# A retention layer with a gated feed-forward behind it, on one core: a new order list for the same operations

## The chip, the core and the metric

The kernel runs on one core of a Trainium2 chip. The metric is device microseconds of one execution. The engines are called as in the profile: PE is the matmul engine (PEld its weight loads), DVE, ACT and POOL work elementwise, and SP only issues transfers here.

## What is computed

Cut from the reference:

```python
# q, k, v: (4 batches, 8 heads, 768 positions, 64)
gamma = 1.0 - 2.0 ** (-5.0 - np.arange(H))
for t in range(S):
    state = gamma[None, :, None, None] * state + np.einsum('bhd,bhe->bhde', k[:, :, t], v[:, :, t])
    y[:, :, t] = (1 / sqrt(D)) * np.einsum('bhd,bhde->bhe', q[:, :, t], state)
x = y.transpose(0, 2, 1, 3).reshape(B * S, H * D)        # 3072 x 512
xn = x / np.sqrt(np.mean(x * x, -1) + 1e-6) * rms_g
g = xn @ w_gate                                          # 512 -> 1536
return (g / (1 + np.exp(-g)) * (xn @ w_val)) @ w_out     # 1536 -> 512
```

The matmuls take bf16 operands and add up in float32; inputs and output are float32.

## The kernel before

The 768 positions are cut into six chunks of 128. Within a chunk and batch, attention is computed as masked scores, and what comes from earlier chunks goes through a state per batch, which each chunk but the last extends. The feed-forward then takes one chunk of all four batches (512 tokens).

Nothing in this kernel is ordered by a scheduler. Every step is a small named function, and a string, ORDER, lists the calls; the last loop (L784) walks through it. A word such as `V.3.3@A` is the step V of chunk 3 and batch 3 on ACT (D is DVE, P is POOL, S is SP), and the digits behind a slash are the PSUM banks it takes, of eight. Each engine executes its instructions in the order of the list and waits where an operand, or the bank or buffer of a result, isn't ready.

The steps, with c the chunk and b the batch:

- `Lq`, `Lk`, `Lv` load; on SP through the hardware queue as float32, on POOL through the software queue with a cast to bf16. `wg`, `wv`, `wo` load pieces of the weights on POOL. Loads of chunk 2 wait for the piece `wo.8` (L327 to L338).
- `Cq`, `Ck` cast q and k, `V` scales v by a decay; on ACT a `V` is eight small instructions, one for each head. `Tq`, `Tk` transpose on PE and `Eq`, `Ek` copy the result out of PSUM (helper L152); for chunk 0 some of them pick rows of a packed layout (L381). From chunk 2 on `tq` and `tk` transpose by a transfer on SP instead (L402).
- `A` is the scores (L418, two array halves of 64 rows), `P` the same with the state's part, `M0` and `M1` apply the mask on DVE, `Y` makes the output rows. `S`, `R`, `N` are the RMS norm (ACT, POOL, DVE), `X` and `XE` its transpose on PE and the copy; `XE@S` is a transfer (L516).
- `J` and `D` make the decayed k, `K` is the state's update (eight products of 64x64, L541, result kv_ps), `U` adds it to the state, `B` casts the state to bf16.
- `g` and `v` are gate and value products (L564), `s` the silu on ACT, `h` the product of both on DVE. Chunk 5 has them in a form with seven products of half blocks (`ga`, `gb`, `gc`, `va`, `vb`, `vc`, L750), which needs sums of weights (`gS`, `vS`) and copies of an accumulator (`gq`, `vq`).
- The output product has the seven-product form in all chunks: `z1` to `z4` and `w1` to `w4` are sums, `a1`, `a6`, `a7`, `a4`, `b2`, `c5`, `c3` products (L660; accumulators a, b, c), `q1`, `q6`, `q7` copies of the accumulator a (tile sn), `r1` to `r4` the four quarters of the result and `s1` to `s4` their stores on SP (L688). An optional last number takes one half of the quarter.
- `H` and `hot` are filler matmuls, which no result uses (hot_ps), `G` and `GE` spread the norm's gain (g_row_ps, g_bc), `tab` is one small activation that brings ACT its table for silu, and `mk0`, `mk1`, `yd`, `vd`, `yt`, `mc` make masks and decays.

```python
    for w in ORDER.split():
        w, _, bk = w.partition("/")
        w, _, en = w.partition("@")
        f, *a = w.split(".")
        F[f](ENG.get(en), [int(i) for i in bk], *map(int, a))
```

Of the kernel before, what the change touches and what calls it, by code (L numbers as in the profile page):

```python
# [17 lines left out]
Lk.0.2@S H.8/0 Lk.1.1@S rms.1@S yt ident iota pick Lk.0.0@P Ck.0.2@D Lq.0.1@P Tk.0.2/1 vd Lq.0.0@P mk1 H.3/2 D.0.2@D  # L18
Lk.0.1@P mk0 Lq.0.2@P Lk.0.3@P Lq.0.3@P Tk.0.0/3 Lv.0.0@P H.1/4 Ek.0.0@D Tq.0.1/5 hot.3/6 Lv.0.1@P J.0.0/7 Eq.0.1@A
Tq.0.0/0 D.0.0@D Lv.0.2@P Eq.0.0@A Tk.0.1/2 Ek.0.2@D H.1/4 Ek.0.1@A Tq.0.2/3 Lv.0.3@P yd hot.2/6 A.0.0/5710 Eq.0.2@D  # L20
tab wg.0.2 G/4 M0.0.0 wv.0.2 M1.0.0 Tq.0.3/2 GE@A wg.2.4 M0.0.1 Tk.0.3/6 Eq.0.3@A Y.0.0/3 M1.0.1 Lq.1.1@P A.0.2/57
Ek.0.3@A H.3/4 M1.0.2 S.0.0 A.0.3/12 M0.0.2 R.0.0 H.1/0 M1.0.3 Y.0.2/6 wv.2.4 K.0.0/4 N.0.0 S.0.2 J.0.1/7 Y.0.1/0
# [796 lines left out]
```

## Time and profile before

| | before |
|---|---|
| times of three runs, us | 228.67, 230.32, 231.47 (median 230.32) |
| span of the profiled execution, us | 228.9 |
| the execution's own time outside the span | not given; the span stands for it |
| granted PE clock | 1.000 of full speed |
| PE busy | 219.0 us, 96% |
| DVE, ACT, POOL busy | 179.8, 98.1, 162.5 us |
| moved by transfers | 33.64 MB, 147 GB/s |
| instructions | 5499 |

Times are those of one profiled execution. A row of a view names the line of the kernel, the engine, the operation and its tiles (out<-in); "xN" is a count, and a bracket tells how long the engine waited ahead of it and for what.

### The profile page before, as it was taken

The numbers are of one execution on the slowest core, as the hardware profiler recorded it, in microseconds if no ns is written. First come the engines' busy times: TensorE is split into PE (matmuls) and PEld (weight loads), VectorE is DVE, ScalarE is ACT, GpSimd is POOL, SyncE is SP. The second block draws the span as 40 slices with busy tenths as digits, with TensorE's granted clock in tenths as the row PEclk, the third lists the DMA queues.
The fourth block names the chain that finished last, engine by engine and source line by source line (L and its number), as shares of the span: only waits on it lengthen the run. The fifth ranks groups of instructions, "written<-read, shape, count | busy, mean of one in ns | idle before, by whom it ended". The sixth has DMA issues, their size and how long they took to land.

```text
span 228.9 us, 5499 instructions
## 1 busy us (share of the span) xinstructions
PE 219.0 (96%) x2119; PEld 145.6 (64%) x2119; DVE 179.8 (79%) x325; ACT 98.1 (43%) x218; POOL 162.5 (71%) x214
## 2 busy tenths in 40 slices
PE   7799989999999999999999999999999999999991
PEld 2568744675447886446574448674457788888871
DVE  6599359889999968679747878791997789999850
ACT  7776342533247252362602424514335328754311
POOL 8979999658998979514584997886198899330800
PEclk9999999999999999999999999999999999999999
DMA  7999999999456888777989579469974432000254
GB/s 134 162 183 131 143 169 177 205 199 241 109 117 138 195 155 171 127 164 172 194 206 204 122 135 259 93 150 226 195 157 157 77 102 92 3 0 3 76 186 153
DMA packets 108171, 33.64 MB, mean 147 GB/s; under 512 B 94449, under 2 KB 108145, under 8 KB 108146
## 3 DMA queue, kind: packets, MB, share of 16 engines
q1 hardware_dynamic: 84674, 25.70, 49.8%
q0 software_dynamic: 23472, 7.60, 30.6%
q8 instruction: 16, 0.26, 0.4%
q14 instruction: 9, 0.07, 0.2%
HBM read 28.31 MB, written 6.29 MB: 151 GB/s over the span
## 4 chain that ended last, share of the span: by engine, by line
PE 59%; ACT 0%; DVE 0%; issue 0%
PE g_ps L564 14%; PE v_ps L564 14%; PE a L660 10%; PE c L660 6%; PE b L660 2%; PE ga L750 2%; PE va L750 2%; PE a_ps L418 1%; PE vc L750 1%; PE gc L750 1%; PE y_ps L456 1%; PE y_ps L460 1%; PE kv_ps L541 1%; PE vb L750 1%; PE gb L750 1%; ACT r L152 0%
## 5 line engine op out<-in xcount | busy, mean ns | idle before, releaser
L574 ACT ACTIVATE sg<-g_ps 128x512 bf16<-128x512 f32 (+2 forms) x64 | 35.9, 570 | 71.1 <-PE g_ps L564 63.2
L564 PE MATMUL g_ps<-xnT,wg_b 128*128 128x512 bf16 (+2 forms) x296 | 58.7, 339 | 0.9 <-ACT xnT L152 0.5
L564 PE MATMUL v_ps<-xnT,wv_b 128*128 128x512 bf16 (+2 forms) x296 | 59.2, 339 | 0.0
L586 DVE TENSOR_TENSOR hT<-sg,v_ps 128x512 bf16<-128x512 bf16 (+2 forms) x64 | 40.1, 647 | 18.7 <-PE v_ps L564 17.5
L564 PEld LDWEIGHTS <-wg_b 128*128 128x128 bf16 x296 | 25.3, 98 | 23.4 <-DMA wg_b<-in_moe_w_gate_dram 0.8
L564 PEld LDWEIGHTS <-wv_b 128*128 128x128 bf16 x296 | 25.6, 98 | 22.3
L660 PEld LDWEIGHTS <-hT 128*128 128x128 bf16 x288 | 27.6, 98 | 4.7
L633 POOL TENSOR_TENSOR z<-hT,z 128x512 bf16<-128x512 bf16 x14 | 16.9, 1218 | 12.7 <-PE a L660 6.7
L660 PEld LDWEIGHTS <-z 128*128 128x128 bf16 x216 | 20.8, 98 | 3.6 <-issue 0.7
L497 DVE SCALAR_TENSOR_TENSOR xn<-y_ps,rstd,g_bc 128x512 bf16<-128x512 f32 x22 | 16.5, 749 | 6.7 <-POOL rstd L485 6.5
L556 POOL CAST st_b<-st_f 64x256 bf16<-64x256 f32 x40 | 20.5, 513 | 1.4
L441 DVE TENSOR_TENSOR am<-a_ps,causal 128x512 bf16<-128x512 f32 x32 | 20.1, 680 | 1.6 <-PE a_ps L418 1.4
L473 ACT ACTIVATE xsq<-y_ps 128x512 bf16<-128x512 f32 x22 | 13.2, 600 | 16.1 <-PE y_ps L460 11.8
L660 PE MATMUL a<-wo_b,hT 128*128 128x256 bf16 x144 | 17.9, 273 | 0.0
L633 POOL TENSOR_TENSOR z<-z,hT 128x512 bf16<-128x512 bf16 x8 | 10.2, 1273 | 7.4 <-DVE z L633 3.8
L485 POOL TENSOR_TENSOR rstd<-ms,mhalf 128x1 f32<-128x1 f32 x24 | 13.7, 570 | 2.0
L483 POOL TENSOR_SCALAR ms<-ssq 128x1 f32<-128x1 f32 x24 | 4.7, 197 | 11.5 <-ACT xsq L473 10.3
L633 POOL TENSOR_TENSOR z<-hT 128x512 bf16<-128x512 bf16 x9 | 10.7, 1190 | 3.0 <-DVE hT L586 2.9
L683 DVE TENSOR_TENSOR r<-c,sn 128x512 f32<-128x512 f32 (+1 forms) x13 | 8.4, 645 | 5.5 <-PE c L660 4.4
L152 ACT COPY sn<-a 128x512 f32<-128x512 f32 x14 | 8.2, 583 | 10.5 <-PE a L660 10.5
L373 POOL TENSOR_TENSOR vp<-vf,vdec 128x512 bf16<-128x512 f32 x11 | 11.5, 1058 | 0.7 <-DMA vf<-in_v_dram 0.7
L441 DVE TENSOR_TENSOR am<-a_ps,mask 128x512 bf16<-128x512 f32 x16 | 10.1, 683 | 0.2 <-PE a_ps L418 0.2
(158 smaller groups left out, 396.0 us busy)
## 6 DMA issues: line engine op xcount, KB each, us to landing
out_dram<-r SPq DMA_DIRECT2D x22, 256.0 KB, 2.4
kf<-in_k_dram SPq DMA_DIRECT2D x18, 256.0 KB, 4.1
qf<-in_q_dram SPq DMA_DIRECT2D x16, 256.0 KB, 3.9
vf<-in_v_dram SPq DMA_DIRECT2D x16, 256.0 KB, 3.7
wo_b<-in_moe_w_out_dram POOLq DMA_DIRECT2D x3, 512.0 KB, 10.0
qb<-in_q_dram POOLq DMA_DIRECT2D x8, 128.0 KB, 5.6
vp<-in_v_dram POOLq DMA_DIRECT2D x8, 128.0 KB, 7.3
kb<-in_k_dram POOLq DMA_DIRECT2D x6, 128.0 KB, 5.1
```

The costliest lines, as they stand in the source:

```text
L373: e.tensor_tensor(out=u["vp"], in0=u["vf"], in1=vdec[:, c, :, None].to_broadcast([128, H, D]), op=ALU.mult)
L441: DVE.tensor_tensor(out=u["am"][:, i], in0=u["a"][i], in1=m, op=ALU.mult)
L473: ACT.activation(xsq, flat(u["y"]), AF.Square, accum_out=u["ssq"])
L485: POOL.tensor_tensor(out=u["rstd"], in0=ms, in1=mhalf, op=ALU.pow)
L497: DVE.scalar_tensor_tensor(out=u["xn"], in0=flat(u["y"]), scalar=u["rstd"], in1=g_bc, op0=ALU.mult, op1=ALU.mult)
L556: POOL.tensor_copy(st_b[b][r, :, i * 64:i * 64 + 64], st_f[b][r])
L564: nc.tensor.matmul(p[:, (n - n0) * m:(n - n0 + 1) * m], W[w][0][:, s, n * 128:(n + 1) * 128], xnT[c][:, s, b0 * C:b1 * C], start=s == 0, s ...
L574: ACT.activation(sg[:, :cols], done["wg", c, n0, b0][:, :cols], AF.Silu)
L586: DVE.tensor_tensor(out=h_of(c, r)[:, i:i + n1 - n0, b0 * C:b1 * C], in0=sg, in1=p, op=ALU.mult)
L633: e.tensor_tensor(out=x, in0=a, in1=b, op=how)
L660: nc.tensor.matmul(done[x, c][:, q], left(i, c, r)[:, k, q * C:q * C + C], right(i)[:, r, k], start=first and q == r == k == 0, stop=r == ...
L750: nc.tensor.matmul(p[:, q], l[:, r, q], m[:, k], start=first and q == k == 0, stop=q == k == 1, skip_group_check=True)
```

## The change

ORDER is replaced by another list. The functions, the loop and the tiles' rings stay. The list has the same steps once each, with one exception: the last accumulation of chunk 4's fourth quarter, its copy and its store (`a4.4.0.3`, `r4.4`, `s4.4`) come in two halves of two batches each. Some steps get another engine, among them `V` (two on ACT before, six after), `Ck`, `Cq`, `XE`, the weight sums and copies. Of the table the diff shows its last lines here:

```diff
-c3.5.2.3.1 r3.5.1 c3.5.2.3.0 r3.5.0 s4.5.1@S s4.5.0@S s3.5.0@S s3.5.1@S b2.5.2.3 r1.5 s1.5@S z4.4.1@P c3.4.0.3 r3.4
-s3.4@S a4.4.0.3 r4.4@A s4.4@S
+r2.4 c3.4.0.3 r4.5.1@A a4.5.2.3.0 r4.5.0@A s4.4.0@S s2.5@S s4.5.1@S s2.4@S z4.5.1@D c3.5.0.2 s4.5.0@S r3.4 c3.5.2.3.1
+r3.5.1 s3.4@S s3.5.1@S a4.4.0.3.1 r4.4.1@A s4.4.1@S c3.5.2.3.0 r3.5.0 s3.5.0@S
```

**State updates (`K`).** PE, where chunk 2's updates stand. kv_ps_1678 is that of `K.2.1` before; what follows it there is a product of chunk 0's output (c).

```order
L541 LDWEIGHTS kb_1353
L541 MATMUL kv_ps_1678<-vp_1597,kb_1353 64x64
L660 LDWEIGHTS z_985
L660 MATMUL c_1687<-w1_1254,z_985 128x256
L660 LDWEIGHTS z_985
L660 MATMUL c_1687<-w1_1254,z_985 128x256
```

PE at that place after: kv_ps_1760 is that of `K.2.3`, kv_ps_1785 that of `K.2.0`.

```order
L541 LDWEIGHTS kb_1381
L541 MATMUL kv_ps_1760<-vp_1422,kb_1381 64x64
L541 LDWEIGHTS kb_1321
L541 MATMUL kv_ps_1785<-vp_1613,kb_1321 64x64
L541 LDWEIGHTS kb_1321
L541 MATMUL kv_ps_1785<-vp_1613,kb_1321 64x64
```

Each of the twenty `K` stood alone among products of full size. From chunk 2 on they now stand in runs: `K.2.3 K.2.0 K.3.3 K.2.1 K.2.2`, then `K.3.2 K.3.1 K.3.0`, `K.4.3` and `K.4.2 K.4.1 K.4.0`; chunk 1's are `K.1.3 K.1.2 K.1.0 K.1.1`.

**The head.** ACT at the start, before, from the masks on. The rows of L302 are `tab`, the casts are copies of transposed q and k.

```order
L284 ACTIVATE mask_101<-row_m,nbias 128x128 x8
L152 CAST qT<-t_ps 128x512 x2
L152 CAST kT<-t_ps 128x512
L278 ACTIVATE ydec<-darg,lnscale 128x48
L302 ACT_TABLE_LOAD
L302 ACTIVATE warm<-zero 128x1
L152 COPY g_bc<-g_row_ps 128x512
```

ACT at the start, after; the rows up to the copy of g_bc, which is followed by more copies, squares and two copies of xnT before the second piece.

```order
L284 ACTIVATE mask_101<-row_m,nbias 128x128 x8
L278 ACTIVATE ydec<-darg,lnscale 128x48
L152 CAST kb<-kf 128x512
L152 COPY kT<-t_ps 128x512
L152 CAST kT<-t_ps 128x512 x2
L152 COPY g_bc<-g_row_ps 128x512
```

```order
L152 COPY xnT<-xt_ps 128x4x128 x2
L574 ACT_TABLE_LOAD
L574 ACTIVATE sg<-g_ps 128x256
L152 COPY kT<-t_ps 128x512
L574 ACTIVATE sg<-g_ps 128x384
```

The load of silu's table moved from the copies of the head to the place just ahead of the first silu (sg), since `tab` now stands in chunk 2. POOL at the start, before: the loads of v, then pieces of the weights among the norms (ms, rstd).

```order
L329 DMA vp<-in_v_dram 128x8x64 x4
L338 DMA wg_b<-in_moe_w_gate_dram 128x4x256
L338 DMA wv_b<-in_moe_w_val_dram 128x4x256
L338 DMA wg_b<-in_moe_w_gate_dram 128x4x256
L329 DMA qb<-in_q_dram 128x8x64
L483 TENSOR_SCALAR ms<-ssq 128x1
```

POOL at the same place after.

```order
L329 DMA vp<-in_v_dram 128x8x64 x4
L338 DMA wv_b<-in_moe_w_val_dram 128x4x256
L338 DMA wg_b<-in_moe_w_gate_dram 128x4x256 x2
L338 DMA wv_b<-in_moe_w_val_dram 128x4x256
L338 DMA wg_b<-in_moe_w_gate_dram 128x4x256
L338 DMA wg_b<-in_moe_w_gate_dram 128x4x384
L483 TENSOR_SCALAR ms<-ssq 128x1
```

Six pieces of the weights are issued ahead of the first norm, where there were three. On PE, 18 of the 20 `H` fillers now stand ahead of the first transposes; they were spread over the head.

**The end.** The last rows of PE before: two products of `c3.4` (c_3735), then the first of the twelve of `a4.4` (a_3687) that end the list.

```order
L660 LDWEIGHTS z_3574
L660 MATMUL c_3735<-wo_b_135,z_3574 128x256
L660 LDWEIGHTS z_3574
L660 MATMUL c_3735<-wo_b_135,z_3574 128x256
L660 LDWEIGHTS hT_2944
L660 MATMUL a_3687<-w4_1380,hT_2944 128x256
```

PE's last rows after: the second half of `a4.4` (a_3663) stands between the halves of `c3.5` (c_3822).

```order
L660 MATMUL c_3822<-wo_b_135,z_3858 128x256
L660 LDWEIGHTS hT_3147
L660 MATMUL a_3663<-w4_1354,hT_3147 128x256
L660 LDWEIGHTS hT_3147
L660 MATMUL a_3663<-w4_1354,hT_3147 128x256
L660 LDWEIGHTS hT_3116
L660 MATMUL a_3663<-w4_1354,hT_3116 128x256
L660 LDWEIGHTS hT_3116
L660 MATMUL a_3663<-w4_1354,hT_3116 128x256
```

SP's last stores before; r_3887 and r_3897 are halves of chunk 5's quarters, the last one is chunk 4's fourth quarter.

```order
L688 DMA out_0_dram<-r_3887 128x256 x2
L688 DMA out_0_dram<-r_3897 128x256 x2
L688 DMA out_0_dram<-r_3910 128x2x256
L688 DMA out_0_dram<-r_3927 128x2x256
L688 DMA out_0_dram<-r_3942 128x2x256
```

SP's last stores after; r_3959 is chunk 5's third quarter, r_3855 chunk 4's fourth.

```order
L688 DMA out_0_dram<-r_3921 128x2x256
L688 DMA out_0_dram<-r_3935 128x256
L688 DMA out_0_dram<-r_3955 128x2x256
L688 DMA out_0_dram<-r_3959 128x256
L688 DMA out_0_dram<-r_3855 128x256
L688 DMA out_0_dram<-r_3959 128x256
```

The last store was a whole quarter of 256 KB; it is a half now, and another half stands ahead of it. Between the head and the end, loads and attention of the later chunks stand earlier among PE's feed-forward products, and the stores of chunks 3 and 4 stand elsewhere among them.

More of the change, by code (lines that the diff above doesn't have):

```diff
@@ L17 @@
 ORDER = """
[L18 to L22, printed above, removed]
@@ L93 @@
-gs1.5.2 ga4.5.0 gs4.5.0 vq1.5.1@A gc3.5.0 gr3.5.0 h.5.0.2.0.2 va6.5.0 vq6.5.0@A ga7.5.1 gq7.5.1@A vb2.5.1/1 vr1.5.1
-vS3.1@P va1.5.2/6 gc5.5.1/4 gs3.5.0 vq1.5.2@A gr2.5.1 gs2.5.1 h.5.4.6.0.2 vb2.5.2/5 va6.5.1 vq6.5.1@A vr1.5.2 z1.4.1@D
-vS3.0@P va7.5.0 ga4.5.1 vc5.5.0/1 z2.4.2@P z4.4.2@P va6.5.2 z2.4.1@P gc3.5.1 va7.5.1 h.5.8.10.0.2 vq7.5.0@A vr2.5.0
-gr3.5.1 gs4.5.1 ga6.5.2 vc5.5.1/5 vq7.5.1@A vr2.5.1 va4.5.0 gs3.5.1 vc3.5.0 a1.5.0.2/0 h.5.2.4.2.4 va4.5.1 vr3.5.0
-a1.5.2.3 h.5.0.2.2.4 h.5.6.8.0.2 vc3.5.1 vr3.5.1 gq6.5.2@A z1.5.0@D vq6.5.2@A va7.5.2 vq7.5.2@A ga7.5.2 h.5.6.8.2.4
@@ L103 @@
-c3.5.2.3.1 r3.5.1 c3.5.2.3.0 r3.5.0 s4.5.1@S s4.5.0@S s3.5.0@S s3.5.1@S b2.5.2.3 r1.5 s1.5@S z4.4.1@P c3.4.0.3 r3.4
-s3.4@S a4.4.0.3 r4.4@A s4.4@S
+yt H.2/0 H.3/1 H.1/2 Lk.1.1@S rms.1@S vd Lq.0.0@P Lk.0.0@P H.8/3 H.3/4 ident pick Lk.0.2@S Lq.0.1@P iota mk0 H.1/5 G/6
+Lk.0.1@P Tq.0.0/7 causal Ck.0.2@D D.0.2@D Tk.0.2/0 Tk.0.0/1 Lq.0.2@P mk1 yd H.1/2 Eq.0.0@D Ck.1.1@A Ek.0.2@A Lk.0.3@P
+Ek.0.0@A Tq.0.1/3 Eq.0.1@D Lq.0.3@P J.0.0/4 D.0.0@D Tk.0.1/5 mc.1@P Ek.0.1@A GE@A hot.2/0 A.0.0/7213 M0.0.0 M1.0.0
@@ new lines @@
+g.0.2.3.0.3/2 s.0.3.4.0.3 R.0.3 N.0.3 s.0.0.2.2.3 v.0.3.4.0.3/3 K.0.3/1 Lq.1.1@P K.0.1/4 X.0.3/6 U.0.3@A XE.0.3@D
+g.0.5.6.0.3/0 g.0.4.5.0.3/1 s.0.2.3.0.3 v.0.2.3.0.3/2 h.0.3.4.0.3 g.0.0.2.1.2/6 g.0.0.4.3.4/3 h.0.2.3.0.3
+v.0.0.4.3.4/2 h.0.0.2.2.3 s.0.0.4.3.4 h.0.0.4.3.4 s.0.4.5.0.3 Tq.1.3/5 Eq.1.3@D g.0.4.6.3.4/3 v.0.4.5.0.3/1
+g.0.9.10.0.4/2 Lk.1.2@P Lk.1.0@P B.0.0 U.0.1@A Tq.1.0/4 s.0.4.6.3.4 s.0.0.2.1.2 h.0.0.2.1.2 v.0.4.6.3.4/3 Tq.1.1/5
+Tk.1.0/6 Lq.1.2@P h.0.4.5.0.3 wv.9.12 Eq.1.0@D h.0.4.6.3.4 g.0.11.12.0.4/7 Lk.1.3@P Eq.1.1@D B.0.3 Ek.1.0@A D.1.2@D
@@ new lines @@
+A.1.0/1436 M1.1.0 v.0.5.6.0.3/5 wg.6.9 Lv.1.3@P Lv.1.1@P mc.0@P Lv.1.0@P s.0.5.6.0.3 h.0.5.6.0.3 wv.6.9 B.0.1 M1.1.1
+M0.1.0 z1.0.0@D Tk.1.2/0 g.0.10.11.0.4/4 s.0.10.11.0.4 v.0.11.12.0.4/5 Tq.1.2/6 Eq.1.2@D Lv.1.2@P Tk.1.3/4
+v.0.10.11.0.4/1 s.0.9.10.0.4 Ek.1.2@A s.0.11.12.0.4 v.0.9.10.0.4/2 M0.1.1 h.0.11.12.0.4 wo.8.12 A.1.2/06 wo.4.8
+Ek.1.3@A A.1.3/73 M1.1.3 wo.0.4 M0.1.3 g.0.8.9.0.4/4 D.1.3@P Lk.2.2@S Y.1.1/5 S.1.1 M1.1.2 B.0.2 g.0.6.7.0.4/3
+h.0.10.11.0.4 Y.1.3/7 S.1.3 s.0.8.9.0.4 D.1.1@P R.1.1 s.0.6.7.0.4 g.0.7.8.0.4/6 Y.1.0/1 S.1.0 R.1.3 M0.1.2 Y.1.2/0
@@ new lines @@
+M0.3.0 R.3.3 Lv.5.1@S Lk.5.3@S a4.1.0.3 M1.3.0 tq.4.2 R.3.1 g.2.11.12.0.4/2 N.3.3 g.2.1.2.0.4/5 Lv.4.1@S Y.3.0/7 N.3.1
+s.2.1.2.0.4 Lq.4.0@S v.2.1.2.0.4/1 gS1.1@P h.2.1.2.0.4 z4.1.0@D S.3.0 R.3.0 N.3.0 Lk.4.3@S z4.1.2@P Cq.4.3@P
+v.2.10.11.0.4/0 tk.4.0 v.2.11.12.0.4/6 z1.2.1@P g.2.8.9.0.4/5 s.2.11.12.0.4 Ck.4.3@A h.2.10.11.0.4 XE.3.1@S
+v.2.3.4.0.4/1 c3.1.0.3 h.2.11.12.0.4 Cq.4.0@P B.3.3 s.2.8.9.0.4 K.3.2/2 K.3.1/7 XE.3.3@S K.3.0/0 U.3.2@D XE.3.0@S
+V.4.0@D V.5.1@A v.2.8.9.0.4/6 h.2.3.4.0.4 r3.1 XE.3.2@S v.2.9.10.0.4/5 g.2.9.10.0.4/2 s.2.9.10.0.4 vS1.1@P U.3.0@D
@@ new lines @@
+v.4.5.6.0.4/0 s4.2@S B.4.2 Y.5.2/3 S.5.2 R.5.2 h.4.7.8.0.4 v.4.9.10.0.4/1 a1.3.0.3/2 h.4.5.6.0.4 s.4.1.2.0.4
+c5.3.0.3/6 gS4.0@D b2.3.0.3/5 vS2.1@D N.5.2 XE.5.1@S z3.3.0@P h.4.1.2.0.4 z1.4.1@P z4.3.0@P z2.4.1@P vS4.1@D
+g.4.9.10.0.4/0 XE.5.2@S XE.5.3@S X3.5@P q1.3@D s.4.9.10.0.4 h.4.9.10.0.4 r1.3 ga1.5.1/4 ga1.5.0/3 a6.3.0.3 q6.3@A
+X1.5@P g.4.8.9.0.4/7 gq1.5.1@A v.4.8.9.0.4/0 s.4.8.9.0.4 gq1.5.0@A gS3.0@D h.4.8.9.0.4 gb2.5.0/1 gr1.5.0 gs1.5.0
+gS4.1@D gb2.5.2/5 vS4.0@D ga1.5.2/7 gq1.5.2@D gS3.1@D a7.3.0.3 q7.3@A gr1.5.2 z4.3.2@D v.4.2.3.0.4/0 gb2.5.1/1 gr1.5.1
@@ new lines @@
+X2.5@P ga6.5.0 gq6.5.0@A r2.3 h.4.2.3.0.4 z3.4.1@D gs1.5.1 a4.3.0.3 va1.5.0/5 z1.4.2@D z2.4.2@D gc5.5.0/1 ga7.5.0
+gq7.5.0@A gr2.5.0 s4.1@S c3.3.0.3 ga6.5.1 gs2.5.0 r3.3 va1.5.1/0 gq6.5.1@D gc3.5.0 gr3.5.0 X4.5@P vb2.5.1/6 ga4.5.0
+vq1.5.0@A ga7.5.1 vS3.0@P vb2.5.0/1 va6.5.0 r4.3@D vS3.1@P vq1.5.1@A gs1.5.2 gc5.5.1/2 vr1.5.1 h.5.4.6.0.2 gs3.5.0
+z4.4.2@P va1.5.2/6 gq7.5.1@A ga4.5.1 vq6.5.0@A vr1.5.0 va7.5.0 vb2.5.2/1 ga6.5.2 gs4.5.1 gr2.5.1 gs2.5.1 gc3.5.1
+h.5.0.2.0.2 gr3.5.1 vc5.5.0/4 vq7.5.0@A va6.5.1 gs4.5.0 gc5.5.2/3 vc5.5.1/2 vr2.5.0 h.5.2.4.2.4 vc3.5.0 vr3.5.0
@@ new lines @@
+h.5.0.2.2.4 gq6.5.2@A vq6.5.1@A va7.5.1 vq1.5.2@A vr1.5.2 z1.4.0@P vq7.5.1@A va6.5.2 z3.4.0@D z2.4.0@P z4.4.0@P s2.3@S
+z3.4.2@P gs3.5.1 va4.5.0 h.5.2.4.0.2 a1.4.0.3/4 ga7.5.2 gq7.5.2@A a1.5.0.2/1 ga4.5.2 vr2.5.1 q1.4@A vc3.5.1 va4.5.1
+gr2.5.2 z1.5.0@D h.5.8.10.0.2 gc3.5.2 vr3.5.1 vq6.5.2@A va7.5.2 vq7.5.2@A z2.5.0@P gr3.5.2 vc5.5.2/5 a1.5.2.3 a6.4.0.3
+h.5.6.8.2.4 b2.4.0.3/2 vr2.5.2 va4.5.2 h.5.4.6.2.4 z1.5.1@D q6.4@A z2.5.1@D vc3.5.2 z3.5.1@D gs2.5.2 h.5.10.12.2.4
+vr3.5.2 h.5.6.8.0.2 q1.5@A a6.5.0.2 gs3.5.2 h.5.8.10.2.4 z4.4.1@P z1.5.2@D z2.5.2@P z3.5.0@P a7.4.0.3 c5.5.0.2/3
```

127 lines of the change are left out of this document (52 added, 75 removed).

## The prediction
> **What bounds the kernel now.** I read the page's busy times first, then the stages, then who makes the matmul engine wait, then the chain that ended last.
>
> ```profile
> PE 219.0 (96%) x2119; PEld 145.6 (64%) x2119; DVE 179.8 (79%) x325; ACT 98.1 (43%) x218; POOL 162.5 (71%) x214
> PE 59%; ACT 0%; DVE 0%; issue 0%
> 30.00:40.00 10.00, 8.93 (x82) 4.34 (x80) 7.13 (x13) 3.38 (x6) 9.84 (x15) 1.00 1.90 172
> 40.00:50.00 10.00, 10.00 (x124) 6.54 (x123) 8.66 (x14) 5.30 (x13) 5.49 (x12) 1.00 1.21 196
> 190.00:200.00 10.00, 10.00 (x94) 8.96 (x93) 9.48 (x16) 8.55 (x17) 6.12 (x6) 1.00 0.16 54
> PE c L660 <- DVE r L683: 0.5, 1, 0.5
> PE kv_ps L541 <- DVE vp L373: 0.4, 1, 0.4
> ```
>
> In the stages, the first number behind the comma is PE's busy time. PE is the bound: from 40 us to about 220 us it is all but full, and the chain runs over PE for as far back as it was followed. PE takes its work in the order of the list. So the end is the sum of PE's slots, plus PE's waits, plus what follows PE's last matmul, and an edit on another engine counts only where PE waits for it. The two waits shown are the ones behind 40 us that are listed for PE's matmuls.
>
> **Tile forms.** K (kv_ps) and the A of attention run in array shapes other than 128x128. Here the chain has two K's among ordinary work (columns: start, length).
>
> ```profile
> 147.51 0.86 PE g_ps L564 x4
> 148.37 0.24 PE kv_ps L541 x8
> 148.62 0.97 PE v_ps L564 x4
> 149.59 0.24 PE kv_ps L541 x8
> 149.83 1.42 PE b L660 x12
> 151.25 1.31 PE c L660 x12
> 8.53 0.44 PE L381 MATMUL t_ps<-pick,qb 128*64 128x64 bf16 x16
> 8.91 0.44 PE L381 MATMUL t_ps<-pick,kb 128*64 128x64 bf16 x16
> ```
>
> Four wide matmuls take 0.86 alone and 0.97 behind a K, twelve products 1.31 alone and 1.42 behind a K. So a lone K costs 0.24 + 0.11 = 0.35 us. A run that stays in K's shape is seen in the last two rows: 16 matmuls from 8.53 to 8.91, which is 0.19 us for eight. A K directly behind another K should cost about that, 0.16 less. The 20 K's stand in 20 places before. After, the 16 from the second chunk on stand in five (runs of 4, 5, 3, 1 and 3), so 11 seams go: 11 x 0.16 = **1.8 us gained**. Bounds: 11 x 0.11 = 1.2 if only the slowed follower is saved, and 11 x 0.24 = 2.6 if a K in a run were nearly free.
>
> **The head, up to 40 us.** Here PE waits for first data and for copies.
>
> ```profile
> 1.11 3.34 PE L252 MATMUL hot_ps<-one 128*128 128x512 bf16 x8 [1.11 <-DVE one L165]
> 4.83 0.81 PE L252 MATMUL hot_ps<-one 128*128 128x512 bf16 x3
> 4.73 2.43 ACT L284 ACTIVATE mask<-row_m,nbias 128x128 f32<-128x128 f32 x8
> 9.49 0.59 ACT L152 CAST kT<-t_ps 128x512 bf16<-128x512 f32 x1
> 9.97 0.35 ACT L278 ACTIVATE ydec<-darg,lnscale 128x48 f32<-128x48 f32 x1
> 10.20 0.62 PE L418 MATMUL a_ps<-qT,kT 64*128 64x128 bf16 x16
> 10.32 1.28 ACT L302 ACT_TABLE_LOAD   x1
> 10.75 1.12 PE L311 MATMUL g_row_ps<-g_row,ones 1*128 1x512 f32 x2
> 16.87 0.63 ACT L152 CAST kb<-kf 128x512 bf16<-128x512 f32 x1
> 23.43 1.50 PE L564 MATMUL g_ps<-xnT,wg_b 128*128 128x128 bf16 x24 [0.47 <-ACT xnT L152]
> 31.84 1.04 PE L564 MATMUL g_ps<-xnT,wg_b 128*128 128x512 bf16 x4 [0.42 <-DMA wg_b<-in_moe_w_gate_dram]
> 33.53 0.40 PE L386 MATMUL t_ps<-ident,qb 128*128 128x128 bf16 x4 [0.65 <-ACT sg L574]
> 33.52 0.23 PEld L386 LDWEIGHTS <-qb 128*128 128x128 bf16 x4 [1.14 <-DMA qb<-in_q_dram]
> ```
>
> Two things get worse. First, 18 of the 20 big filler matmuls (hot_ps) now stand at the very start: eight slow ones to 4.5 and ten of about 0.2 us end near 6.6, and the g_row product (1.1) runs to 7.7. On ACT, masks to 7.2 are followed by ydec (0.35), a cast (0.63) and two kT copies (0.59 each), to about 9.6, since the second one's transpose ends near 8.9. J.0.0, which needs that copy, now stands on PE ahead of Tk.0.1: 9.6, J 0.25, the transpose 0.4, one more copy 0.6 and some hand-overs give a first A near 11.1 instead of 10.20, 0.9 late. Second, the table load (1.28) leaves its hidden place and stands directly ahead of the first silu, whose PSUM bank the second v product behind it wants: PE waits about 1.1.
>
> Two things get better. Five of the weight pieces and wg.9 are issued ahead of the first rstd pair on POOL, and all of chunk 1's q ahead of wv.9, so the DMA waits at 31.84 and 33.53 (0.42 and 0.65) should go, and with other work ahead the one at 23.43 (0.47). A matmul's row runs about 0.17 past its slot (1.04 here, 0.86 in the chain), so each gap really costs that much more: 1.54 + 3 x 0.17 = 2.0. Sum 0.9 + 1.1 - 2.0 = 0, and two seams fewer there: **-0.3 us**. Bounds: -2.0 (the new waits are covered) and +2.0 (the old ones stay).
>
> **The full stretch.** The wait for V.3.3 (0.4) should go: it stands behind two K's now. New waits come, because PE's order leaves less room. An example: the copy of an accumulator (sn) between product 7 and product 4 of one bank.
>
> ```profile
> 203.50 0.44 PE ga L750 x4
> 206.12 0.44 PE ga L750 x4
> L152 ACT COPY sn<-a 128x512 f32<-128x512 f32 x14 | 8.2, 583 | 10.5 <-PE a L660 10.5
> ```
>
> Before, ga7 ends at 203.9 and ga4 starts at 206.1: 2.2 us for a copy of 0.58. After, two products of 0.44 stand between: 0.87. Going through both lists with such durations I find some 30 places with under 0.9 us to spare, where before had four; none is short by itself, so only a busy queue makes PE wait there. Bounds 0 and +3 (0.1 at each); I take **+0.6**, somewhat over a wait like the two of before. With the -0.4: +0.2. Four V's more on ACT, eight small ACTIVATEs each, are some 8 us on an engine that is 43% busy: no term.
>
> **The end.**
>
> ```profile
> 220.35 0.42 DVE L683 TENSOR_TENSOR r<-c,sn 128x256 f32<-128x256 f32 x1 [1.38 <-PE c L660]
> 220.82 0.38 PE L660 MATMUL c<-wo_b,z 128*128 128x256 bf16 x2 [0.52 <-DVE r L683]
> 222.95 1.32 PE a L660 x12
> 224.30 0.58 ACT L152 COPY r<-a 128x512 f32<-128x512 f32 x1 [3.80 <-PE a L660]
> out_dram<-r SPq DMA_DIRECT2D x22, 256.0 KB, 2.4
> out_dram<-r SPq DMA_DIRECT2D x4, 128.0 KB, 1.7
> ```
>
> PE waits 0.52 between the halves of c3 of chunk 5, because r3.5.1 reads the bank that the second half writes. After, six matmuls of a4 (half of 1.32) stand between: **-0.5 us**. The last result was a whole one: copy 0.58, then 2.4 to landing. Now it is a half: 0.42, then 1.7; -0.9 at most. Another half store is issued just ahead, so I take **-0.8** (bounds -0.9 and 0, the latter if the stores queue). The Trainium skill, "DMA: Bandwidth & Descriptors", section "Anatomy of one DMA — SWDGE (gpsimd) path", speaks against much gain from halving: about 2 us are fixed and bytes cost 1 us per 436 KB, 0.3 us for 128 KB. By that the sum would be 0.4 less; it was fitted on the other path, and the rows here show 0.7.
>
> **Sum**: -1.8 - 0.3 + 0.2 - 0.5 - 0.8 = -3.2 us, from a span of 228.9 to 225.7. The median of the three times, 230.32, lies 1.4 above that span; carried over, **227.1 us**. A change under 1% (2.3 us) can't be told from none on this kernel.
>
> **Rivals.**
>
> *The gain is eaten* by the tight places: +3 instead of +0.6 leaves -0.8, 229.5 us. For it: DVE is 95% busy from 190 to 200 us. Against: one wait gives room to all behind it. Chance 0.20.
>
> *The change doesn't do what it says*: K's side by side still cost 0.35, since each has a bank of its own. Then -1.4 is left, 228.9 us. Against: the two transposes in a row also change banks. Chance 0.07.
>
> *SP's queue becomes the bound: slower.* By the PE work ahead of it, A.5.0 comes some 18 us sooner, while no load is fewer.
>
> ```profile
> SPq L329 <- DMA wo_b<-in_moe_w_out_dram: 46.1, 1, 46.1
> 79.98 7.05 SPq L516 DMA_TRANSPOSE xnT<-xn  x4
> 96.09 1.22 SPq L402 DMA_TRANSPOSE qT<-qb  x1
> ```
>
> SP's loads from chunk 2 on start when a piece of wo has landed, after a wait of 46.1 us, near 48.6. Until A.5.0 it issues 47 loads, 44 transposes and 7 stores. At some 0.6, 1.22 and 0.5 us that is 85 us; A.5.0 would stand near 154, 105 us later. If every transpose took the slow 1.76 (7.05 for four), it is 109 us and 4 us late; with the waits for casts between them PE would stand still at the last A's for some 8 us in all, 235 us. It decides where SP's issue and waits exceed 105 us. Against: wo's third piece is issued first now, which starts SP some 4 us earlier. Chance 0.08.
>
> *PE's clock falls in the head*, since the fillers leave the gaps from 9 to 17 us: the first rows of the head show 0.42 us for a slow filler. One stretch of 3.4 us at half speed would cost 1.7, 228.8 us. The Trainium skill, "TensorE: Matmul & The Clock Gate", section "HAM oscillation — how this bites in real kernels", sets this at idle gaps over about 3.4 us; no gap in my walk is over 1.2. Chance 0.03.
>
> *More is gained*: the head ends 2.0 ahead and nothing new waits, 224.8 us. Chance 0.15.
>
> **How the numbers follow.** The forecast has the remaining 0.47, from 225.6 to 228.8. The better cases reach down to 223.9 (K at its bound of 2.6 besides), the eaten gain up to 230.5 where tight places cost 4. Range **223.7 to 230.6**: outside lie the SP case and a little on either side. Faster by over 1% means under 228.0: 0.15, some 0.35 of the forecast and 0.06 of the rivals, **0.56**. Slower by over 1%, over 232.6: the SP case and 0.01 besides, **0.09**. Within 1%: **0.35**.
>
> **What would show it.** Right: K's in a run at about 0.2 us each; the table load just ahead of the first silu and a PE wait of about 1 us near 22; no DMA among PE's waits from 25 to 40; no wait between the halves of c3; 0.8 us less between PE's last matmul and the end. Wrong: PE waiting for transposed q or k behind 90 us, or waits of PE over 2 us in the full stretch.

## The result, and the profile after

The new list is slower: 238.07 us median (237.88 to 239.23, four runs) against 230.49 before (four runs, one more than the three of the 230.32 above); the ratio is 1.036, interval 1.031 to 1.041. The profiled execution took 238.14 us with a span of 236.4, so 7.5 us more span than before.

Busy times and the shares of the chain that ended last, of the page after:

```profile
PE 221.3 (94%) x2119; PEld 147.1 (62%) x2119; DVE 182.7 (77%) x324; ACT 107.3 (45%) x256; POOL 148.2 (63%) x206
PE 51%; DVE 19%; POOL 9%; DMA 9%; issue 6%; ACT 3%; SPq 2%; POOLq 0%; DVEq 0%; ACTq 0%
```

Before, the chain named PE and next to nothing else, but it was followed back only to about 89 us. After, it is followed to the start and half of it lies elsewhere. Part of that half is the head, which the chain of before doesn't reach, so the two shares can't be set side by side; behind 89 us too, though, it now passes through DMA, DVE and POOL. Where PE stands still, the busy time by stages tells; first before, then after (stretch, its length, then PE's busy time):

```profile
0.00:40.00 40.00, 35.71 (x485) 22.71 (x486) 28.89 (x77) 22.46 (x52) 36.90 (x62) 1.00 1.52 157
80.00:120.00 40.00, 39.59 (x368) 24.50 (x366) 28.89 (x49) 15.63 (x38) 24.52 (x38) 1.00 0.82 170
```

```profile
0.00:40.00 40.00, 36.32 (x490) 23.43 (x491) 26.97 (x74) 23.39 (x54) 37.91 (x65) 1.00 1.57 167
40.00:80.00 40.00, 39.62 (x391) 25.36 (x390) 36.46 (x59) 18.98 (x47) 29.12 (x38) 1.00 0.99 203
80.00:120.00 40.00, 38.53 (x339) 24.16 (x337) 28.42 (x48) 16.87 (x46) 22.12 (x34) 0.96 0.86 172
120.00:160.00 40.00, 37.44 (x330) 22.21 (x328) 29.59 (x52) 15.63 (x42) 25.16 (x38) 1.00 0.75 165
160.00:180.00 20.00, 19.66 (x147) 10.23 (x145) 15.40 (x26) 9.71 (x26) 6.75 (x14) 1.00 0.24 67
180.00:210.00 30.00, 27.32 (x230) 22.17 (x229) 27.51 (x39) 13.93 (x27) 20.65 (x17) 1.00 0.17 54
```

In the head PE is idle for 3.7 us instead of 4.3. From 40 to 210 us it was idle for 0.4 before, all of it in the stretch shown; after, it is idle for 0.4 + 1.5 + 2.6 + 0.3 + 2.7 = 7.4. What PE waits for, after (the rows that the text uses; others of up to 1.1 us are not shown):

```profile
PE gc L750 <- DVE vf L762: 1.2, 1, 1.2
PE a_ps L418 <- DMA qT<-qb: 1.1, 3, 0.6
PE g_ps L564 <- DMA xnT<-xn: 1.0, 1, 1.0
PE v_ps L564 <- ACT sg L574: 1.0, 1, 1.0
PE vb L750 <- DVE vf L762: 0.7, 1, 0.7
PE kv_ps L541 <- POOL vp L373: 0.6, 1, 0.6
PE va L750 <- DVE vf L762: 0.5, 1, 0.5
```

Three of these name what SP transposes (qT, xnT) or what stands behind a late load (vp), and three name the vector engine's sums of chunk 5 (vf); the wait for sg is one of the head. So behind the head there are two groups: one up to 160 us, one from 180 to 205.

**SP.** Its own instructions after, near the longest wait for xnT (start, length):

```profile
122.67 0.46 SPq L329 DMA_DIRECT2D qf<-in_q_dram  x1
123.17 0.72 SPq L329 DMA_DIRECT2D kf<-in_k_dram  x1
123.99 2.97 SPq L402 DMA_TRANSPOSE qT<-qb  x1
127.07 0.53 SPq L329 DMA_DIRECT2D qf<-in_q_dram  x1
127.69 0.53 SPq L329 DMA_DIRECT2D vf<-in_v_dram  x1
128.31 0.97 SPq L329 DMA_DIRECT2D kf<-in_k_dram  x1
```

Each starts about 0.1 us behind the end of the one before it. It is so from 44.3 to 159.5 us: 98 transfers, with one pause of over 0.3 (0.5). Before, pauses of over 0.3 add up to 14 us between 57 and 160. One of 1.6 us, from 90.2 to 91.8, in the same view of before:

```profile
89.25 0.94 SPq L329 DMA_DIRECT2D vf<-in_v_dram  x1
91.76 1.62 SPq L402 DMA_TRANSPOSE qT<-qb  x1
```

SP has become an engine that is always busy, though no page counts its issuing as busy time.

**The stretch at K.3.3.** PE and, below, ACT:

```profile
83.59 0.44 PE L541 MATMUL kv_ps<-vp,kb 128*64 128x64 bf16 x16
84.27 2.49 PE L541 MATMUL kv_ps<-vp,kb 128*64 128x64 bf16 x24 [0.23 <-ACT vp L371]
86.69 2.74 PE L660 MATMUL c<-wo_b,z 128*128 128x256 bf16 x12
```

```profile
83.35 0.62 ACT L152 CAST kb<-kf 128x512 bf16<-128x512 f32 x1 [3.54 <-DMA kf<-in_k_dram]
83.87 2.02 ACT L371 ACTIVATE vp<-vf,vdec 128x64 bf16<-128x64 f32 x8
```

V.3.3 stands on ACT behind a cast that waits 3.54 us for a load from SP, and K.3.3 gets its eight rows one by one, 0.24 apart. Three K's take 2.49 us, and the 12 products behind them take 2.74, where the same view has 1.47 for twelve (at 228.94, below): the stage from 80 to 120 us has a granted clock of 0.96, since the clock was halved for 3.4 us from 86.5 on. The stages count all this as busy, so it comes on top of the 7.4.

**DVE.** The sums of chunk 5's weights between 179 and 195 us, after, by kind:

```profile
L715 DVE TENSOR_TENSOR kf<-wv_b,vf 128x768 bf16<-128x768 bf16 x2 | 2.9, 1432 | 0.0
L715 DVE TENSOR_TENSOR wg_b<-wg_b 128x768 bf16<-128x768 bf16 x2 | 1.9, 966 | 0.0
L715 DVE TENSOR_TENSOR vf<-vf,wv_b 128x768 bf16<-128x768 bf16 x1 | 1.5, 1511 | 0.0
L715 DVE TENSOR_TENSOR kf<-wg_b,qf 128x768 bf16<-128x768 bf16 x2 | 1.4, 708 | 0.0
```

Seven sums, 7.7 us. Before, DVE had none of them in that stretch: POOL did five of the seven, from 53 us on, and DVE two at 131 and 176.

### The profile page after: what moved, and what is told of

Same layout as the page of the kernel before. It is cut to its first block, busy times and chain, and to the rows that moved or that the text cites. A ratio compares the mean times of both kernels' runs of the same rounds, so it can differ in the third digit from the quotient of the medians.

```text
span 236.4 us, 5515 instructions
## 1 busy us (share of the span) xinstructions
PE 221.3 (94%) x2119; PEld 147.1 (62%) x2119; DVE 182.7 (77%) x324; ACT 107.3 (45%) x256; POOL 148.2 (63%) x206
## 4 chain that ended last, share of the span: by engine, by line
PE 51%; DVE 19%; POOL 9%; DMA 9%; issue 6%; ACT 3%; SPq 2%; POOLq 0%; DVEq 0%; ACTq 0%
PE g_ps L564 14%; PE v_ps L564 12%; PE a L660 8%; PE c L660 5%; DVE hT L586 4%; DMA kf<-in_k_dram 3%; DMA qf<-in_q_dram 3%; DMA qT<-qb 3%; DVE vf L762 2%; DVE w L618 2%; PE b L660 2%; POOL vp L329 2%; DVE z L633 2%; DVE r L683 1%; PE y_ps L456 1%
## 5 line engine op out<-in xcount | busy, mean ns | idle before, releaser
L586 DVE TENSOR_TENSOR hT<-sg,v_ps 128x512 bf16<-128x512 bf16 (+2 forms) x64 | 40.8, 648 | 27.7 <-PE v_ps L564 19.6
L574 ACT ACTIVATE sg<-g_ps 128x512 bf16<-128x512 f32 (+2 forms) x64 | 35.1, 569 | 58.1 <-PE g_ps L564 45.5
L660 PEld LDWEIGHTS <-z 128*128 128x128 bf16 x216 | 21.6, 102 | 5.1 <-issue 0.5
L633 POOL TENSOR_TENSOR z<-z,hT 128x512 bf16<-128x512 bf16 x10 | 13.3, 1335 | 14.7 <-PE vc L750 8.2
L556 POOL CAST st_b<-st_f 64x256 bf16<-64x256 f32 x40 | 17.7, 442 | 6.3 <-DVE st_f L549 4.9
L354 POOL TENSOR_TENSOR qb<-qf,ydec 128x512 bf16<-128x512 f32 x9 | 9.9, 1106 | 15.2 <-DMA qf<-in_q_dram 14.0
L152 ACT COPY sn<-a 128x512 f32<-128x512 f32 x16 | 9.3, 584 | 20.6 <-PE a L660 19.0
L633 POOL TENSOR_TENSOR z<-hT,z 128x512 bf16<-128x512 bf16 x11 | 13.7, 1249 | 5.1 <-DVE z L633 3.3
L371 ACT ACTIVATE vp<-vf,vdec 128x64 bf16<-128x64 f32 x48 | 12.0, 336 | 0.0
L418 PE MATMUL a_ps<-qT,kT 64*128 64x128 bf16 x192 | 8.8, 218 | 2.4 <-DMA qT<-qb 1.1
```

What stands on the lines that cost most here:

```text
L371: ACT.activation(u["vp"][:, h], u["vf"][:, h], AF.Copy, scale=vdec[:, c, h:h + 1])
L556: POOL.tensor_copy(st_b[b][r, :, i * 64:i * 64 + 64], st_f[b][r])
L574: ACT.activation(sg[:, :cols], done["wg", c, n0, b0][:, :cols], AF.Silu)
L586: DVE.tensor_tensor(out=h_of(c, r)[:, i:i + n1 - n0, b0 * C:b1 * C], in0=sg, in1=p, op=ALU.mult)
L633: e.tensor_tensor(out=x, in0=a, in1=b, op=how)
L660: nc.tensor.matmul(done[x, c][:, q], left(i, c, r)[:, k, q * C:q * C + C], right(i)[:, r, k], start=first and q == r == k == 0, stop=r == ...
```

## The experiments

Two theories stood against each other: that SP's queue sets PE's pace up to 160 us and DVE from 180 on, or that single steps stand in wrong places, each costing what PE waits there. In some of the kernels below the list takes one line less, and line numbers are one lower than elsewhere; in those of the seventh they are three higher.

**1. V.3.3 ahead of the cast.**

```diff
-Ck.3.2@A V.3.3@A
+V.3.3@A Ck.3.2@A
```

> After, with one pair on ACT exchanged: V.3.3 stands ahead of Ck.3.2, which waits for a load until 83.3 us, so K.3.3 no longer gets its rows one head at a time. The theory 'SP's queue sets the pace' (SP issues without a pause from 45 to 160 us): the stretch of about 2.4 us at K.3.3 goes, with the slow products behind it, but PE then waits as much longer at the next transposes (A.3.2, the first product on chunk 3's xnT, K.4.3): 238.1 falls by 0 to 1 us. The rival 'each wait is a local misplacement': it falls by 2.5 us or, with the slow products of that profile, by 4.

Measured: 236.6 us, ratio to before 1.032 (1.027 to 1.036). In this kernel K.3.3 doesn't wait. The scores of chunk 3, its row and then that of after:

```profile
104.82 0.86 PE L417 MATMUL a_ps<-qT,kT 64*128 64x128 bf16 x16 [1.89 <-DMA qT<-qb]
```

```profile
105.70 0.40 PE L418 MATMUL a_ps<-qT,kT 64*128 64x128 bf16 x8 [0.58 <-DMA qT<-qb]
```

PE comes to the scores more than 2 us sooner and starts them 0.9 sooner; the rest is waited for there (1.89 instead of 0.58). At the first product of chunk 3 almost nothing is left of it: that starts at 122.5 us here and at 122.8 after. What was 3 to 4 us in its place is 1.5 us by the medians and about 1 in the ratio. That lies between what the two theories said (0 to 1, and 2.5 to 4), and the intervals of this kernel and of after overlap, so the time alone decides nothing. The trace leans to the queue, with a reservation: the profiled execution was the slowest of its four, and behind the wait of 1.89 it has a half clock of its own, for 3.4 us.

**2. Loads of v from ACT.**

```diff
-Lv.3.0@S ... Lv.5.3@S
+Lv.3.0@A ... Lv.5.3@A
```

> After, with the 12 loads of v of chunks 3 to 5 issued from ACT instead of SP, at the same places of the list. SP is spared 12 x 0.76 = 9 us of issues between 70 and 165 us. 'SP's queue sets the pace': SP shows pauses, the waits for qT, xnT and k of chunk 3 go, and the time falls by 3 to 5 us, to 233 to 235. 'Local misplacement' or 'DVE alone': within 1 us of 238.1. What may spoil it: ACT, at the place of a load, waits for a free buffer, and silus are late behind it.

Measured: 231.93 us, ratio 1.011 (1.006 to 1.015): by the ratios 5.8 us of the 8.3 are gone, more than expected, only by who issues twelve loads. PE's busy time in the two stages:

```profile
80.00:120.00 40.00, 38.10 (x347) 23.50 (x346) 29.35 (x53) 18.30 (x50) 23.30 (x34) 1.00 1.08 193
120.00:160.00 40.00, 39.66 (x354) 23.48 (x353) 32.19 (x55) 15.40 (x40) 25.44 (x39) 1.00 0.81 158
```

PE's idle time from 120 to 160 falls from 2.6 to 0.3, and K.3.3 doesn't wait in this execution, whose clock stays at 1.00 in both stages. Of 6.4 us of span, 2.7 are idle time of PE and 3.8 busy time, most of it that of K.3.3 and the slow products behind it. The bytes are the same, so it was SP's queue and not the bandwidth. The loads left SP's instructions and SP's queue of transfers at once, so the run doesn't tell apart the time to issue them from the backlog of that queue.

**3. Four sums on POOL.**

```diff
-vS2.1@D ... vS4.1@D ... gS4.1@D ... vS4.0@D
+B.4.1 vS2.1@P vS4.1@P vS4.0@P gS4.1@P
```

> After, with four sums of weights for chunk 5 (vS2.1, vS4.1, vS4.0, gS4.1; 5.2 us on DVE between 180 and 193 us) on POOL, into its idle stretch from 162 to 171 us. 'DVE is the second bound, from 180 to 205 us': PE's waits of 0.5, 0.7, 1.3 and 0.8 us there shrink by 2 to 3 us in all, 235 to 236 us. Rival 'these waits are what the late SP queue hands on': no more than 0.5 us, since the feed-forward's own sums on DVE stay late.

Measured: 233.73 us, ratio 1.020 (1.016 to 1.024). The stage with the sums:

```profile
180.00:210.00 30.00, 29.75 (x258) 24.92 (x256) 25.44 (x41) 15.86 (x29) 19.12 (x16) 1.00 0.18 54
```

PE is idle there for 0.25 us instead of 2.7. That is 2.4 of the 4.4 us of span that this execution gained. The other 2.0 lie ahead of that stage: K.3.3 still gets its rows one by one, but the clock is not halved behind it. So this edit is worth about 2.4 us by the trace, within the 2 to 3 expected.

**4. The table early.**

```diff
-z2.1.1@P tab Ck.3.2@A
+yd tab
```

> After, with the load of silu's table back among the copies of the head (behind the activation that makes ydec). The wait of PE at the first v product behind the first silu (1.2 us near 21.9) goes, but 1.28 us more stand ahead of the first copies of k. 'SP's queue sets the pace': SP's stretch starts with the landing of a weight piece that POOL issues, so a head that PE ends 1 us sooner is waited for again behind 65 us: within 0.5 us of 238.1. 'Every wait of PE counts by itself': 1 us less, or nothing if the copies are late.

Measured: 237.27 us, ratio 1.033 (1.029 to 1.038), not to be told from after. The wait of PE behind the first silu (1.0) is gone. Behind 60 us the waits for SP have grown instead:

```profile
PE a_ps L418 <- DMA qT<-qb: 3.7, 4, 1.5
PE g_ps L564 <- DMA xnT<-xn: 1.9, 2, 1.2
```

After, these rows say 1.1 and 1.0. At chunk 2's scores, near 67 us, PE comes 1.0 us sooner and waits 1.2 for qT, so that microsecond is waited for behind the head, at the full queue. The rest of the growth is another thing: K.3.3 is slow here too, but no half clock follows it, and the 1.4 us that PE is ahead at 89 us are waited for at 105.

**5. All four at once.**

```diff
-Lv.3.0@S ... Lv.5.3@S ... Ck.3.2@A V.3.3@A ... vS2.1@D vS4.1@D gS4.1@D vS4.0@D
+yd tab ... Lv.3.0@A ... Lv.5.3@A ... V.3.3@A Ck.3.2@A ... B.4.1 vS2.1@P vS4.1@P vS4.0@P gS4.1@P
```

> After with all four edits at once: loads of v of chunks 3 to 5 from ACT, the four sums on POOL, V.3.3 ahead of Ck.3.2, silu's table early. Theory 'two bounds one behind the other, SP up to 160 us and DVE from 180 to 205 us': the gains of both add up, 6 us and 3 us (of the 4.3 that the sums gave alone, the part behind 180 us), and the early table now counts with about 1 us, since SP no longer sets the pace: 227 to 229 us. Rival 'one bound, seen in two places': no better than the better single edit, 231 to 232.

Measured: 229.8 us, ratio 0.9965 (0.9932 to 0.9997): better than any single edit, so there are two bounds, one behind the other. It is a little above the 227 to 229 that I expected. Two waits are among the reasons, a new one for a reader on ACT and a longer one for xnT, now near 90 us:

```profile
PE kv_ps L541 <- ACT r L152: 2.0, 1, 2.0
PE g_ps L564 <- DMA xnT<-xn: 1.3, 1, 1.3
```

**6. SP started early.** The wait of chunk 2's loads for a piece of w_out is taken out.

```diff
-            after(i, ("wo", 8))
+            pass
```

> After, where SP's loads of chunk 2 no longer wait for the landing of a piece of w_out: SP starts them in the head instead of near 45 us, with the same instructions in the same order. SP can run ahead until its buffers are full (some ten loads, 7 us of issues) or until a transpose waits for its cast. 'SP's queue sets the pace up to 160 us': what SP gains at its start is gained at PE's waits behind 80 us, 3 to 6 us, to 232 to 235, less what the loads cost the weights in the head. Rival 'the transfers' own bandwidth sets the pace, not the queue': the bytes are the same, and the time stays within 1 us of 238.

Measured: 243.93 us, ratio 1.059 (1.053 to 1.066), 6 us slower than after: a miss. SP's instructions in the head, and the stage from 10 to 20 us, first here, then after:

```profile
14.44 2.41 SPq L328 DMA_DIRECT2D qf<-in_q_dram  x1
16.95 3.01 SPq L328 DMA_DIRECT2D kf<-in_k_dram  x1
20.00 42.78 SPq L328 DMA_DIRECT2D qf<-in_q_dram  x2
```

```profile
10.00:20.00 10.00, 6.90 (x161) 5.00 (x156) 6.52 (x11) 4.71 (x11) 6.27 (x11) 0.79 1.65 181
```

```profile
10.00:20.00 10.00, 8.56 (x201) 6.61 (x199) 8.59 (x14) 6.80 (x17) 9.51 (x17) 1.00 1.66 163
```

SP ran only eight loads ahead and then stood until 62 us, for a buffer that a cast on DVE frees (the last row counts the eighth load and the one behind that standstill as one). These loads took 0.6 to 5.4 us each, most of them 2.4 to 3.4. The first loads of the head came later: up to 40 us PE now waits 3.5 us for loads of v and 1.0 for pieces of w_gate, neither of which after has. In the stage shown PE is idle for 3.1 us of ten instead of 1.4 and its clock falls to 0.79; in the next it is 0.70. So this run says nothing for or against the queue; it shows what the wait for w_out is good for.

**7. The same load more on both.** Behind each load of v of chunks 3 to 5 stands another one on SP, which nothing reads.

```diff
+            if n == "v" and c >= 3:
+                more = const.tile([128, H, 2], F32, name=f"more{c}{b}")
+                e.dma_start(out=more, in_=rows[n][b, c][:, :, :2])
```

> Before, with 12 small loads more on SP: behind each load of v of chunks 3 to 5 a second one of its first two columns (128x8x2), which nothing reads. At some 0.5 us of issue each, SP has 6 to 8 us more to do between 70 and 165 us. 'SP's queue is the bound in the new order only': before, SP stood still for 19 us of these, which takes up the added ones, and the time stays within 1 us of 230.2. Rival 'SP is as near its limit in both orders': 3 us slower or more.

> After, with the same 12 small loads more on SP. 'SP's queue is the bound': every issue pushes the next transposes back, and PE waits as much longer: 5 to 8 us slower than after, 243 to 246. Rival 'SP is only busy, and PE waits for something else': within 1 us of 238.

Measured: before with it 234.62 us, ratio 1.024 (1.017 to 1.030); after with it 244.87, ratio 1.066 (1.061 to 1.071). After pays 6.8 us, as expected. Its waits for what SP transposes, which were 1.1 and 1.0:

```profile
PE a_ps L421 <- DMA qT<-qb: 3.4, 4, 1.3
PE g_ps L567 <- DMA xnT<-xn: 2.1, 1, 2.1
```

Of its 6.6 us of span, 4.9 are idle time of PE between 40 and 180 us; another part is a second stretch at half clock, near 128 us. The added loads carry 8 KB each and took SP 11 us, so it is their number that costs, and not their bytes. Before pays 4.4, which I had not expected. I had put SP's pauses there at 19 us; those of over 0.3 between 70 and 165 us are 8.4, and the added loads took 10.1. So the old order was already near the limit, and the new one crossed it.

**8. The single gains, on before.** First the end, then K's in runs.

```diff
-c3.5.2.3.1 r3.5.1 c3.5.2.3.0 ... a4.4.0.3 r4.4@A s4.4@S
+c3.5.2.3.1 r3.5.1 b2.5.2.3 r1.5 c3.5.2.3.0 ... a4.4.0.3.0 r4.4.0@A s4.4.0@S a4.4.0.3.1 r4.4.1@A s4.4.1@S
```

```diff
-K.2.1/3 c5.0.0.3/7 ... K.2.0/6 a4.0.0.3 ... K.2.3/1 ... K.2.2/4
+c5.0.0.3/7 ... a4.0.0.3 ... K.2.1/3 K.2.0/6 K.2.3/1 K.2.2/4 ... K.3.1/6 K.3.0/7 ... K.4.3/3 K.4.1/5 ... K.4.0/7 K.4.2/3
```

> Before, with the end alone changed as the new list changes it: the last quarter result of chunk 4 in two halves, and the four products b2.5.2.3 between the halves of c3 of chunk 5. My terms: 0.5 us for the wait between the halves, 0.8 for the smaller last store: -1.3 us by the profile. Rival: the stores queue behind each other and only 0.5 is left.

> Before, with K's put together and nothing else moved than the U that reads each: K.2.1, K.2.0, K.2.3, K.2.2 in one run, K.3.1 with K.3.0, K.4.3 with K.4.1, K.4.0 with K.4.2: six seams fewer. By my term 6 x 0.16 = 1.0 us less; bounds 0.7 and 1.4. Rival: the grouped K's wait for operands or banks that a lone K did not wait for, and the time doesn't fall.

In the new list the other half of a4 stands between the halves of c3; here b2.5.2.3 does, so this is the same idea and not the same order.

Measured: 229.46 us, ratio 0.998 (0.995 to 1.002), and 229.49, ratio 0.997 (0.994 to 1.001). Neither is clear of no change, and the 1.3 us hoped for at the end lie outside the first interval. The end still has a wait of its own, since the second half of a4 writes the bank that r4.4.0 reads; and the run of K's made the next product wait for a bank. The end, then the K's:

```profile
222.38 0.81 PE L660 MATMUL a<-w,hT 128*128 128x256 bf16 x6 [0.46 <-ACT r L152]
```

```profile
82.40 0.84 PE L540 MATMUL kv_ps<-vp,kb 128*64 128x64 bf16 x32
84.76 0.49 PE L659 MATMUL b<-wo_b,hT 128*128 128x256 bf16 x3 [1.52 <-DVE st_f L548]
118.66 0.37 PE kv_ps L540 x16
```

The runs themselves are as cheap as hoped (two K's in 0.37 in the chain); the wait of 1.52 is more than the 1.0 us that all six seams should bring.

**9. Versions that gather the gains.** Both edits on before with a mask's half moved behind loads in the head, and then with other banks and turns that take those two waits away (the mask not moved):

```diff
-K.2.1/3 K.2.0/6 K.2.3/1 K.2.2/4 ... b2.5.2.3 r1.5 c3.5.2.3.0 ... a4.4.0.3.0 r4.4.0@A s4.4.0@S a4.4.0.3.1
+K.2.0/6 K.2.3/1 K.2.1/4 K.2.2/5 ... a4.4.0.3.0 r4.4.0@A c3.5.2.3.0 r3.5.0 ... b2.5.2.3 r1.5 ... c3.4.0.3 r3.4 ... a4.4.0.3.1
```

> Before with the two edits above and one more in the head: the second half of the mask for chunk 1 (mc.1, 1.1 us on POOL) stands behind the loads of q and the piece wv.9.12 instead of ahead of Lq.1.0. Terms: -1.3 for the end, -1.0 for the K's, and up to -0.7 for the wait on a load of q at 33.5 us, where it comes about 0.3 to 1 us sooner: 226.8 to 228 us, with SP's queue as little in the way as before. Rival: the waits of the head are only moved and 228.5 is left.

> Before with K's in runs as above but in other banks, so that the next product (b2.1.0.3) no longer waits 1.6 us for the reader of K.2.1, and with an end in which each half of a bank is read while PE works in another bank (a4.4's halves and c3.5's take turns), so that its waits of 0.24 and 0.62 us go. Terms: K's -1.0, the wait in c3 -0.5, the last store -0.8: 227.9 us or a little less. Rival: the reader of a run's last K is late for the next tile of its bank, 229.

Measured: 229.12 us, ratio 0.997 (0.995 to 0.999), and 229.39, ratio 0.996 (0.993 to 0.999). Both beat before, by 0.3 to 0.4%, narrowly clear of no change; of the 2.3 us of my terms 0.9 is seen in the second (0.2 to 1.6). And on after, the four edits and these, then (not shown) five loads of q on ACT, two loads of chunk 3 later, and V.4.3 ahead of a cast:

```diff
-Lq.4.2@S ... XE.2.0@S ... V.3.3@A Ck.3.2@A ... r4.0@A
+XE.2.0@S Lq.4.2@S ... r4.0@A V.3.3@A Ck.3.2@A
```

> The four edits to after together, and two more on the path that was left: PE waited 2.2 us at K.2.1 for its bank, whose reader r4.0 stood on ACT behind a cast that waits for a load, and 1.4 us for chunk 2's xnT. r4.0 stands ahead of that cast now, and one load of q (chunk 4) behind the four transposes of xnT instead of among them. By these two waits, up to 3.6 us less than 229.8: 226.5 to 228. Rival: SP's queue sets the pace there too, and the waits come back at the next scores: 229.

> The best version of after so far (228.9), with five loads of q more on ACT, two loads of chunk 3 behind the transposes of chunk 2 that the first scores wait for, and V.4.3 ahead of a cast on POOL that waits for a load. PE's waits there were 1.0 (scores of chunk 2), 0.9 (scores of chunk 3) and 1.4 us (K.4.3): 226 to 227.5. Rival: with that much moved, ACT's loads wait for buffers and silus are late, 229 or more.

Measured: 228.93 us, ratio 0.993 (0.990 to 0.997), the lowest time of all, though not clear of the 229.12 and 229.39 above; with more moved 230.15, ratio 1.001 (0.997 to 1.004), although its profiled execution has the shortest span of all, 226.3. Why its other executions took longer stays open.

## Why the prediction was wrong, by its own steps

**K's in runs: right.** After, the chain has

```profile
50.08 0.64 PE kv_ps L541 x32
153.59 0.50 PE kv_ps L541 x24
```

four K's in 0.64 and three in 0.50, 0.16 to 0.17 each, where I had taken 0.19 and a lone one costs 0.35.

**The head: right in its main terms, and near in the sum partly by luck.** The wait for the table came (1.0 at 21.9 us, forecast 1.1) and the three waits for loads and xnT went. But the first A came 0.5 us late instead of 0.9, at 10.7, and two waits came that I did not have (0.6 for am, 0.5 for xn). PE's idle time up to 40 us fell by 0.6; forecast -0.3.

**The end: right in both terms.** There is no wait between the halves of c3 of chunk 5; from PE's last rows:

```profile
228.94 1.47 PE L660 MATMUL c<-wo_b,z 128*128 128x256 bf16 x12
...
231.56 0.82 PE L660 MATMUL a<-w,hT 128*128 128x256 bf16 x6
232.24 0.38 PE L660 MATMUL c<-wo_b,z 128*128 128x256 bf16 x2
```

From the last row's end, 232.6, to the span's end are 3.8 us; before, from the end of a4 near 224.3, 4.6. That is the 0.8.

**The full stretch: this step failed.** I had +0.2 and the runs show 7 us of waits and some 3 of the stretch at K.3.3. It failed in three ways.

First, the rival of SP's queue was the right one, and I gave it a chance of 0.08 because its term was mis-sized. I had 47 loads, 44 transposes and 7 stores at 0.6, 1.22 and 0.5, which makes 85 us, and said it decides where issue and waits exceed 105. After, the 47 loads took 37.5 us (0.80 each), the transposes 65.2 (1.48), the stores 4.6 (0.66), and the 97 gaps between them about 0.08 each, 7.8 in all: 115 us. The gaps were to be seen before, and so were slow transposes: of 18 behind a load, 8 took 1.6 to 3.1 us. Also, A.5.0 did not come 18 us sooner, at 154, but 10 sooner, at 161.7 instead of 172.2, since PE stood waiting on the way. The rival's price was 235 us; 238.1 were measured, with the sums of the next paragraph in it, which that price did not have. The Trainium skill, "DMA: Bandwidth & Descriptors", section "Issuing engines are not separate DMA queues", says that starting DMAs from several engines only saves the sequencer's time to start them, usually small. The twelve loads of the second experiment show that here it was not small: moved off SP they gave back some 6 us of 238, whether by their issue or by the backlog of SP's queue.

Second, I went through the engines that the list gives each step, but priced only V's. Seven sums landed on DVE in the stretch where I had noted DVE as 95% busy, five of them from POOL, 7.7 us in all (5.8 for the five). By the third experiment PE idles 2.4 us less in that stage without four of them.

Third, I let the wait for V.3.3 go because V.3.3 stood behind two K's. I didn't ask what stands ahead of it on ACT. It is a cast that waits for SP.

The half clock was a rival too, in the head, where no gap of mine was long enough. It came at K.3.3, where PE is never idle for more than 0.24 us but gets one small product each 0.24 us, for 2 us. The Trainium skill, "TensorE: Matmul & The Clock Gate", section "HAM oscillation — how this bites in real kernels", speaks of idle gaps over about 3.4 us; no gap of PE here was near that, and 3.4 us at half clock followed all the same. The same slow K.3.3 in the third and fourth experiments was not followed by one, so what halves the clock stays open. It isn't the cause of the result: three more executions of after had a mean granted clock of 0.998 to 1.000 and took 237.9 to 239.2 us.

## What to carry to other kernels

An engine that only issues transfers can be the bound without a row that says so: add up its issues, with the gaps between them, against the time until the last consumer, and price each kind of issue by what stands ahead of it. Little slack is soon used up: before's pauses add up to 8.4 us, and 10.1 us of added loads cost 4.4. When a list moves steps between engines, price each move on the engine that receives it, in the stretch where it lands. A wait that is removed ahead of a full queue can be waited for again behind it, as the microsecond of the early table was by its trace, so look for the queue first.

## What the runs showed of the hardware

In after, a transpose on SP took 1.22 us (the median) behind another transpose, and behind a load 1.59, up to 3.0 (at 123.99 above, where the two loads ahead of it landed only after its issue had ended). A load on SP took 0.57 us (the median) behind 60 us and up to 2.0. Issued early in the head, in the sixth experiment, most took 2.4 to 3.4 us.

In after, PE got one small product each 0.24 us for 2 us at K.3.3, and 3.4 us at half clock followed. In the runs of the third and fourth experiments nearly the same stretch was not followed by one.
